# The first 256 tokens' softmax rebuilt, one more unit with narrow attention products, and a new order: a chunked-attention and channel-mix kernel on one core

## The chip, the cores and the metric

The kernel runs on one core of a Trainium2 chip. The metric is device time in microseconds (us), given as the median of several runs. A run that was recorded by the hardware profiler has a time of its own; its span, from the first to the last recorded instruction, is somewhat shorter than that time.

The engines are called as in the profile: PE (TensorE) multiplies matrices and PEld loads its weights, DVE (VectorE) does elementwise work, reductions and 32x32 transposes, ACT (ScalarE) evaluates functions and copies, POOL (GpSimd) does little here, and SP (SyncE) issues all DMA transfers through one queue, in program order.

## The reference

Inputs: q, k, v of shape (4, 8, 768, 64), eight memory keys and values per head, two mixing vectors and three weight matrices. The first half is attention in chunks of 32 tokens, each with 16 tokens of left context, 8 of right context and the 8 memory keys (64 keys in all); the second half is a channel mix with a gate.

```python
for c in range(nc):                       # 24 chunks of 32
    q_c = q[:, :, c_start:c_end]
    k_full = np.concatenate([mem_k, k[:, :, l_start:r_end]], axis=2)
    v_full = np.concatenate([mem_v, v[:, :, l_start:r_end]], axis=2)
    scores = scale * np.matmul(q_c, k_full.transpose(0, 1, 3, 2))
    scores = scores - np.max(scores, axis=-1, keepdims=True)
    a = np.exp(scores)
    a = a / (np.sum(a, axis=-1, keepdims=True) + 1e-09)
    out[:, :, c_start:c_end] = np.matmul(a, v_full)
x = out.transpose(0, 2, 1, 3).reshape(4, 768, 512)
x_prev = np.concatenate([zeros, x[:, :-1, :]], axis=1)
xk = mu_k * x + (1.0 - mu_k) * x_prev     # xr in the same way with mu_r
k = np.maximum(xk @ w_k, 0.0)             # w_k: 512 x 1024
v = k * k @ w_v                           # w_v: 1024 x 512
r = 1.0 / (1.0 + np.exp(-(xr @ w_r)))     # w_r: 512 x 512
return r * v
```

## The kernel before

**Tiles and stages.** The 3072 tokens are 12 units of 256, each of two tiles of 128 tokens (tiles 0 and 1 are unit 0, and so on). For a tile PE makes the scores s in PSUM (64 small matmuls), DVE takes the maximum of each row (mx), subtracts it (e), ACT takes the exponential of e in place, DVE sums, adds 1e-9, takes the reciprocal and multiplies ("norm"). For units 0 to 2 PE transposes e (pt, line 751), ACT and DVE copy the two halves into a zeroed block layout (aTz), and PE multiplies by v (px, line 771: 16 calls of two passes for a tile, the "wide" product). From unit 3 (MOVED) on, DVE transposes e in 32x32 blocks (eT, L900), it goes to DRAM (eD, L907) and comes back as aTz in four transfers (L911). From unit 6 (ROWX) on, px is one "narrow" product of 64 matmuls for both tiles (L843), which DVE transposes (f_turn, L850) and which comes back as xT through DRAM too (xD L856, xT L861).

From xT ACT and DVE make the two token mixes (xf: "own" on ACT, L950, and "past" on DVE, L958, for unit 0), split into a high and a low part (xh, xl). PE then makes k (ph, h in the tables of the order), the gate (pr, g) and the value products (pv, v; from unit 2 on seven products p1 to p7 into accx, accy, accz). ACT squares the relu (kf), DVE and ACT split it (ah, al), and the result o goes out.

**Weights.** Each weight arrives as 64-bit words (raw) and is joined once: ACT "abs" (L465), DVE "low" (L470), DVE "join" (L474), then a high and a low part. w0 to w3 are w_k's four blocks of 128 rows, w4 and w5 hold w_r, w6 to w9 w_v. The first product of unit 0 (ph, L1425) takes w0 as joined, with xf.

**What sets the order.** A planner (class Plan) has a cost for each operation, runs the list against its model of the engines, and writes each engine's program in the order found. LEAD lists PE's work of the first two units by hand, STAGES that of the later ones: t is a tile's transposes, a its px, s and z scores of a unit two or three ahead, x and a the px of later units. LOADS is the order of the first transfers. FORCE adds dependencies in unit 0: n, norm of tile 0 waits for the subtraction of tile 1; j, the join of w0 waits for norm of tile 1; t, the copies of tile 1's aTz both go to ACT; e would hold abs behind tile 1's exponential. FETCH and its kin model stops of PE's own instruction queue. While PE would idle before the first ph it multiplies zeros ("warm", L1639).

**The lines of unit 0.** Tile 0 is done by first_part in two halves (q0a, q0b): scores L670, maxima L679 and L681, subtraction L688 and L690, exponential L693, sums L699, L701, L702, norm L706. Tile 1 goes whole through the general path: scores L588, maximum L601, subtraction L606, exponential L612, sums L616 to L618, norm L622.

## Time and profile before

| what | us |
|---|---|
| median of 3 runs | 377.25 (374.96 to 377.32) |
| the profiled execution's own time | 376.67 |
| its span | 374.9 |
| PE busy | 367.7 (98% of the span) |
| DVE busy | 322.7 (86%) |
| ACT busy | 206.2 (55%) |
| DMA | 64.78 MB, mean 173 GB/s |

The granted TensorE clock is full in all 40 slices of the span. "Busy" is the time in which an engine has an instruction at work; for PE that includes the warm matmuls of the head. The profiled execution took 0.58 us less than the median of the runs shown.

### The profile page before, as it was taken

What the parts mean: (1) busy time and instruction counts of PE and PEld (TensorE: products, weight loads), DVE (VectorE), ACT (ScalarE), POOL (GpSimd) and SP (SyncE); (2) the same over time, 40 slices, a digit from 0 to 9 for tenths busy, and PEclk for the clock granted to TensorE, in tenths of its full rate; (3) what the DMA queues carried; (4) which work ended last, traced back from release to release, by engine and by line L of the source; (5) the groups of instructions that cost most, each with busy time, mean ns of one, the idle gap of its engine ahead of it and who ended that gap; (6) DMA issues with size and microseconds to landing.
All of it is one profiled execution on the core that took longest, in us unless ns stands there. A gap on an engine that the chain in (4) does not pass through costs nothing.

```text
span 374.9 us, 11497 instructions
## 1 busy us (share of the span) xinstructions
PE 367.7 (98%) x5084; PEld 339.6 (91%) x5084; DVE 322.7 (86%) x524; ACT 206.2 (55%) x307; POOL 2.4 (1%) x9
## 2 busy tenths in 40 slices
PE   7999999999999999999999999999999999999996
PEld 5886579988999999999999998999999999999996
DVE  3899999999999499989699997996998988788274
ACT  2797996954774386475068157238338244156260
POOL 2000000000000000000000000000000000000000
PEclk9999999999999999999999999999999999999999
DMA  7999981324701735556692485266343340400101
GB/s 287 403 417 409 389 309 71 113 87 140 274 39 72 262 120 179 215 165 240 246 278 93 153 288 179 64 220 230 127 154 115 112 169 2 143 30 0 58 1 58
DMA packets 24146, 64.78 MB, mean 173 GB/s; under 512 B 2720, under 2 KB 10784, under 8 KB 23712
## 3 DMA queue, kind: packets, MB, share of 16 engines
q1 hardware_dynamic: 24096, 64.04, 47.8%
q8 instruction: 40, 0.66, 0.7%
q14 instruction: 10, 0.08, 0.1%
HBM read 49.88 MB, written 14.16 MB: 171 GB/s over the span
## 4 chain that ended last, share of the span: by engine, by line
PE 82%; DMA 9%; DVE 5%; SPq 1%; issue 1%; ACT 0%; DVEq 0%
PE ph L1479 26%; PE pr L1368 14%; PE accy L1270 10%; PE accx L1270 7%; PE accz L1270 6%; PE pv L1581 4%; DMA raw<-in_w_k_dram 4%; PE s L588 4%; PE ph L1454 3%; PE px L771 3%; PE px L843 2%; PE pv L1568 2%; DMA qk<-in_qk_dram 2%; DMA aTz<-eD 1%; DMA xT<-xD 1%
## 5 line engine op out<-in xcount | busy, mean ns | idle before, releaser
L1479 PE MATMUL ph<-xh,wk 128*128 128x256 f32 x320 | 89.1, 278 | 0.0
L1479 PE MATMUL ph<-xh,wl 128*128 128x256 f32 x320 | 88.0, 275 | 0.0
L1479 PE MATMUL ph<-xl,wk 128*128 128x256 f32 x320 | 88.0, 275 | 0.0
L1498 ACT ACTIVATE kf<-ph 128x512 f32<-128x512 f32 x47 | 27.6, 596 | 88.7 <-PE ph L1479 88.4
L1479 PEld LDWEIGHTS ph<-xh,wk 128*128 128x128 f32 x320 | 61.4, 192 | 0.8
L1479 PEld LDWEIGHTS ph<-xh,wl 128*128 128x128 f32 x320 | 61.5, 192 | 0.0
L1479 PEld LDWEIGHTS ph<-xl,wk 128*128 128x128 f32 x320 | 61.4, 192 | 0.0
L1215 DVE TENSOR_TENSOR al<-kf,ah 128x512 fp32r<-128x512 f32 x50 | 33.6, 679 | 1.8 <-PE accz L1270 1.6
L1368 PE MATMUL pr<-wr,xh 128*128 128x512 f32 x88 | 34.1, 388 | 0.0
L1368 PE MATMUL pr<-wr,xl 128*128 128x512 f32 x88 | 33.4, 379 | 0.0
L1368 PE MATMUL pr<-wl,xh 128*128 128x512 f32 x88 | 33.4, 379 | 0.0
L397 ACT CAST ah<-kf 128x512 fp32r<-128x512 f32 x45 | 27.3, 620 | 9.7 <-DVE kf L1193 7.2
L1505 ACT ACTIVATE kf<-kf 128x512 f32<-128x512 f32 x45 | 28.1, 632 | 1.1
L1377 ACT ACTIVATE sg_sb<-pr 128x512 f32<-128x512 f32 x24 | 14.0, 597 | 20.5 <-PE pr L1368 20.3
L1270 PE MATMUL accx<-wv,ah 128*128 128x256 f32 x80 | 22.1, 276 | 0.0
L1270 PE MATMUL accx<-wv,al 128*128 128x256 f32 x80 | 22.0, 275 | 0.0
L1270 PE MATMUL accx<-wl,ah 128*128 128x256 f32 x80 | 22.0, 275 | 0.0
L588 PEld LDWEIGHTS s<-qk 64*32 64x32 f32 x1472 | 15.2, 105 | 4.0 <-issue 2.9
L1368 PEld LDWEIGHTS pr<-wr,xh 128*128 128x128 f32 x88 | 16.7, 189 | 2.5
L1368 PEld LDWEIGHTS pr<-wr,xl 128*128 128x128 f32 x88 | 16.6, 189 | 2.3
L1368 PEld LDWEIGHTS pr<-wl,xh 128*128 128x128 f32 x88 | 16.7, 189 | 1.9
L588 PE MATMUL s<-qk 64*32 64x64 f32 x1472 | 17.2, 225 | 1.1 <-DMA qk<-in_qk_dram 1.1
(165 smaller groups left out, 956.0 us busy)
## 6 DMA issues: line engine op xcount, KB each, us to landing
qk<-in_qk_dram SPq DMA_DIRECT2D x23, 768.0 KB, 6.1
vw<-in_vw_dram SPq DMA_DIRECT2D x24, 512.0 KB, 5.2
out_dram<-o SPq DMA_DIRECT2D x23, 256.0 KB, 2.4
eD<-eT SPq DMA_DIRECT2D x9, 512.0 KB, 2.7
aTz<-eD SPq DMA_DIRECT2D x36, 128.0 KB, 3.0
raw<-in_w_v_dram SPq DMA_DIRECT2D x4, 1024.0 KB, 10.2
raw<-in_w_k_dram SPq DMA_DIRECT2D x3, 1024.0 KB, 10.6
xD<-aTz SPq DMA_DIRECT2D x6, 512.0 KB, 2.6
```

Of the source, the lines that this page charges most:

```text
L397: e.copy(dst, src)
L588: nc.tensor.matmul(s5[CHUNK * j : CHUNK * (j + 1), h, d - c, r, :], *operands(ts[d], r, j, slice(64 * h, 64 * h + 64)), start=True, stop=True,
L771: nc.tensor.matmul(p3[64 * h : 64 * h + 64, 2 * g : 2 * g + 2, CHUNK * j : CHUNK * j + CHUNK], v[:, g, h, j, :], a[:, h, g, j, :], start=True,
L1215: nc.vector.tensor_sub(low(n), place[n](), T["ah", u, n].bitcast(F32))
L1270: nc.tensor.matmul(o, x, w, start=(n in fresh and c + i == 0), stop=(c == cs[-1] and i == 2), skip_group_check=True)
L1368: nc.tensor.matmul(pairs(p), x[:, place_of(u)[k], c * P : (c + 1) * P], woven(w), start=(k + n == 0), stop=(k == KT - 1 and n == 2),)
L1377: nc.scalar.activation(sg, p, AF.Sigmoid)
L1454: nc.tensor.matmul(pairs(T["ph", u, f][:, i * UTOK : (i + 1) * UTOK]), w[:, fc], x[:, :, k].rearrange("p t n -> p n t"), start=(i + k + n ...
L1479: nc.tensor.matmul(pairs(p[:, i * UTOK : (i + 1) * UTOK]), w[:, fc], x[:, :, place_of(u)[k]].rearrange("p t n -> p n t"), start=(k + n == ...
L1498: e.activation(part(), p, AF.Relu)
L1505: e.activation(q, q, AF.Square)
L1581: nc.tensor.matmul(pairs(p), x[:, tc_], woven(w), start=(f + n == 0), stop=(f == FT - 1 and n == 2),)
```

## The change

In the first_part of the new kernel:

- Tile 0 is FUSED: DVE takes the maxima and multiplies them by -SCALE; ACT then takes the exponential straight from PSUM in eight instructions of 128 x 64, each with its own column of maxima as bias and with the row sum as a second output (accum_out). DVE's two subtractions and two sums of tile 0 are gone.
- Tile 1 is loaded in two halves (q1a, q1b) and goes through maxima, subtraction, exponential and sum in two halves.
- Tile 0's scores lie in two banks of tag m and two of tag tp.

Beyond first_part: FORCE is "njc" (c makes w0's abs wait for tile 0's copies; t is gone, so one of tile 1's copies may go to DVE); ROWX is 5, so unit 5 has the narrow px; LOADS, LEAD and STAGES are new, and so is the model of queue stops and one more kind of edge when the order is written (a slot's opener behind its last opener).

```diff
-FORCE = "njt"
+FORCE = "njc"
-LOADS = "q0a q0b q1 id w0 v0 v1 w1a w1b w2 w4 w3 q3 q2 w5 w6 v2 w7 w8 v3 q4 w9 q5"
+FUSED, FUSED_US = (0,), 1.2
+LOADS = "q0a q0b q1a q1b w0 id v0 v1 w1a w1b w2 w3 q2 w4 q3 w5 w6 w7 v2 w8 w9 v3 q4 q5"
 STAGES = {
...
-    10: "h0 h1 h2 h3 p1 p7 g0 p6 p4 p5 p2 p3",
+    9: "h0 h1 x h2 h3 p1 z g0 p7 p6 g1 p5 p2 p4 p3",
+    10: "h0 h1 h2 h3 g0 p1 p7 p6 p4 p5 p2 p3",
...
-ROWX = 6
+ROWX = 5
...
-FETCH, FETCH_LEAD, FETCH_US, FETCH_AT, FETCH_FROM, FETCH_RATE = 256, 40, 4.9, 123, 2600, (0.0046, 0.0088)
+FETCH, FETCH_LEAD, FETCH_US, FETCH_AT, FETCH_FROM, FETCH_RATE = 256, 32, 4.0, 123, 2600, (0.0046, 0.0088)
...
+                elif k > b:
+                    marks[b] = max(marks.get(b, 0.0), ready)
...
+                if s.tag in opened and opened[s.tag] is not o:
+                    edge(opened[s.tag], o)
+                opened[s.tag] = o
...
+            def f_sub(b):
+                if fused:
+                    nc.vector.tensor_scalar_mul(mxs(b), mxs(b), -SCALE)
+                    return
...
+            def f_exp(b):
+                if not fused:
+                    nc.scalar.activation(e4(b), e4(b), AF.Exp, scale=SCALE)
+                    return
...
+                for h in range(2):
+                    for r in range(R):
+                        g = slice(R * b + r, R * b + r + 1)
+                        nc.scalar.activation(
+                            e4(b)[:, h, r], s4(b, h)[:, r], AF.Exp, bias=pt["mx"][:, h, g], scale=SCALE, accum_out=pt["sum"][:, h, g]
+                        )
...
+            es_, banks = [], [[Slot("s")]] * 2 if t else [[Slot("m"), Slot("m")], [Slot("tp"), Slot("tp")]]
```

How the engines' programs stand before and after, at three places. In the names, e is the exponentials' tile, s_0_0 to s_0_3 are tile 0's score banks, mx_0, sum_0 belong to tile 0, mx_1, sum_1, s_1 to tile 1; a wait is named by the engine whose count is waited for.

ACT at the start of the program, before:

```order
L693 ACT_TABLE_LOAD
L693 ACTIVATE e_136<-e_136 128x2x128 [waits DVE_49] x2
L612 ACTIVATE e_136<-e_136 128x2x256 [waits DVE_49]
L465 ACTIVATE w_208<-raw_187 128x512 [waits DMAHW5_49]
L397 COPY aTz<-pt_199 64x512 [waits PE_49]
L397 COPY aTz<-pt_199 64x512
L465 ACTIVATE w_208<-raw_187 128x512
L397 COPY aTz<-pt_223 64x512 [waits PE_49]
L397 COPY aTz<-pt_223 64x512
```

and after (the rows left out are the second instruction of each pair and one abs with its copy):

```order
L715 ACT_TABLE_LOAD [waits DVE_49]
L715 ACTIVATE e_140,sum_0_139<-s_0_0_92,mx_0_117 128x64 [waits PE_49]
L715 ACTIVATE e_140,sum_0_139<-s_0_0_92,mx_0_117 128x64
L715 ACTIVATE e_140,sum_0_139<-s_0_1_94,mx_0_117 128x64 [waits PE_49]
...
L715 ACTIVATE e_140,sum_0_139<-s_0_2_96,mx_0_117 128x64 [waits DVE_49,PE_49]
...
L715 ACTIVATE e_140,sum_0_139<-s_0_3_98,mx_0_117 128x64 [waits PE_49]
...
L706 ACTIVATE e_140<-e_140 128x2x128 [waits DVE_49] x2
L473 ACTIVATE w_218<-raw_188 128x512 [waits DMAHW4_49]
L405 COPY aTz<-pt_208 64x512 [waits PE_49]
...
L405 COPY aTz<-pt_224 64x512 [waits DVE_49]
```

The table load, which stood unwaited, now stands behind a wait for DVE; two exponentials of tile 0 have become eight that read PSUM; tile 1's has become two of half the width; and one copy of tile 1's aTz is left on ACT, behind a DVE instruction.

DVE from the last step of tile 0's softmax to w0's join, before (two sums of tile 0 stand ahead, L699):

```order
L601 TENSOR_REDUCE mx_1_189<-s_1_148 128x8 [waits PE_49]
L606 TENSOR_TENSOR e_136<-s_1_148,mx_1_189 128x2x256 [waits DVE_49]
L706 TENSOR_TENSOR e_136<-e_136,sum_0_143 128x2x256
L616 TENSOR_REDUCE sum_1_204<-e_136 128x8 [waits Activation_49]
L617 TENSOR_SCALAR sum_1_204<-sum_1_204 128x8 [waits DVE_49]
L618 RECIPROCAL sum_1_204<-sum_1_204 128x8 [waits DVE_49]
L622 TENSOR_TENSOR e_136<-e_136,sum_1_204 128x2x256 [waits DVE_49]
L470 TENSOR_SCALAR raw_187<-raw_187 128x1024 [waits DMAHW5_49]
L474 SCALAR_TENSOR_TENSOR w_208<-w_208,raw_187 128x1024 [waits DVE_49,Activation_49]
```

and after (six maxima, two scalings and tile 1's first subtraction stand ahead):

```order
L726 TENSOR_SCALAR sum_0_139<-sum_0_139 128x8 [waits Activation_49]
L727 RECIPROCAL sum_0_139<-sum_0_139 128x8 [waits DVE_49]
L700 TENSOR_TENSOR e_140<-s_1_147,mx_1_170 128x2x128
L724 TENSOR_REDUCE sum_1_200<-e_140 128x2x2 [waits Activation_49]
L731 TENSOR_TENSOR e_140<-e_140,sum_0_139 128x2x256 [waits DVE_49]
L724 TENSOR_REDUCE sum_1_200<-e_140 128x2x2 [waits Activation_49]
L726 TENSOR_SCALAR sum_1_200<-sum_1_200 128x8 [waits DVE_49]
L727 RECIPROCAL sum_1_200<-sum_1_200 128x8 [waits DVE_49]
L731 TENSOR_TENSOR e_140<-e_140,sum_1_200 128x2x256 [waits DVE_49]
L478 TENSOR_SCALAR raw_188<-raw_188 128x1024 [waits DMAHW4_49]
L407 COPY aTz<-pt_224 64x512 [waits PE_49]
L482 SCALAR_TENSOR_TENSOR w_218<-w_218,raw_188 128x1024 [waits DVE_49,Activation_49]
```

Tile 0's add and reciprocal now wait for ACT and stand between tile 1's two subtractions; tile 1's steps come in halves; a copy of aTz (L407) stands between low and join.

SP where unit 8's probabilities go to DRAM and come back, before (eD_3206 and aTz; qk are later score operands):

```order
L907 DMA eD_3206<-eT_3204 128x1024
L561 DMA qk_3212<-in_qk_dram 128x1536
L911 DMA aTz<-eD_3206 32x4x256 x4
L561 DMA qk_3297<-in_qk_dram 128x1536
L745 DMA vw_3307<-in_vw_dram 128x1024
...
L856 DMA xD_3369<-aTz 128x1024
```

and after (eD_3214 is the same transfer):

```order
L945 DMA eD_3214<-eT_3211 128x1024
L1353 DMA out_dram<-o_0_2810 128x512
L949 DMA aTz<-eD_3214 32x4x256 x4
L569 DMA qk_3235<-in_qk_dram 128x1536
...
L783 DMA vw_3377<-in_vw_dram 128x1024
...
L894 DMA xD_3418<-aTz 128x1024
```

The qk load that stood between eD and the four aTz transfers now stands behind them, and an output stands there.

PE in unit 1 and 2, at the transposes and products of tiles 4 and 5 (pt_830, px_860 are tile 4; pt_836, px_885 tile 5; of the twelve ph rows between, four are shown), before:

```order
L751 MATMUL pt_830<-id_sb,e_738 128x128 x4
L751 MATMUL pt_836<-id_sb,e_738 128x128 x4
L1454 MATMUL ph_2_780<-xh_0_683,wk_71 128x256
L1454 MATMUL ph_2_780<-xl_0_685,wk_71 128x256
L1454 MATMUL ph_2_780<-xh_0_683,wl_736 128x256
...
L1454 MATMUL ph_3_787<-xh_0_683,wk_71 128x256
...
L771 MATMUL px_860<-aTz,vw_571 64x2x32 x16
L771 MATMUL px_885<-aTz,vw_575 64x2x32 x16
L1368 MATMUL pr_0_909<-wr_76,xh_1_772 128x512
```

and after (pt_952 is tile 5's transposes, px_959 and px_987 are the products of tiles 4 and 5; tile 4's transposes stand 27 rows higher up):

```order
L1406 MATMUL pr_0_929<-wr_77,xh_1_797 128x512
L1406 MATMUL pr_0_929<-wl_909,xh_1_797 128x512
L1406 MATMUL pr_0_929<-wr_77,xl_1_840 128x512
L789 MATMUL pt_952<-id_sb,e_745 128x128 x4
L809 MATMUL px_959<-aTz,vw_656 64x2x32 x16
L809 MATMUL px_987<-aTz,vw_658 64x2x32 x16
L1619 MATMUL pv_0_1007<-wv_72,kh_0_829 128x512
L1619 MATMUL pv_0_1007<-wl_942,kh_0_829 128x512
```

The twelve ph products that stood between tile 5's transposes and the px products are ahead of the transposes now.

## Rows read from the trace of the kernel before

**Rows 1.** Busy time by stretch: from:to, length, then PE, PEld, DVE, ACT, POOL

```profile
0.00:16.56 16.56, 13.87 (x229) 10.62 (x229) 9.54 (x25) 6.97 (x12) 2.33 (x8) 1.00 0.90 338
16.56:220.00 203.44, 203.33 (x2950) 183.54 (x2947) 188.58 (x287) 129.34 (x191) 0.11 (x1) 1.00 0.58 208
220.00:226.00 6.00, 4.82 (x55) 4.50 (x62) 4.58 (x9) 4.21 (x8) 0.00 (x0) 1.00 0.69 211
226.00:374.90 148.90, 145.71 (x1870) 140.97 (x1868) 119.99 (x206) 65.69 (x99) 0.00 (x0) 1.00 0.31 104
```

**Rows 2.** Waits from 220 to 228: total us, times, longest

```profile
PE px L843 <- DMA aTz<-eD: 1.2, 2, 0.6
```

**Rows 3.** SP's transfers around unit 8's eD: start, us of issuing

```profile
215.22 0.33 SPq L907 DMA_DIRECT2D eD<-eT  x1
215.60 0.45 SPq L561 DMA_DIRECT2D qk<-in_qk_dram  x1
218.12 2.88 SPq L911 DMA_DIRECT2D aTz<-eD  x4
```

**Rows 4.** The chain that ended last, in order of time: start, us, piece

```profile
1.64 6.87 DMA qk<-in_qk_dram
...
67.23 1.34 PE ph L1454 x12
68.58 2.02 PE px L771 x64
...
174.06 1.41 PE px L843 x89
...
220.56 5.28 DMA aTz<-eD
```

**Rows 5.** The timeline of the first 17 us: start, us, instruction [idle before]

```profile
0.73 1.28 ACT L693 ACT_TABLE_LOAD   x1 [0.73 <-PEq L1685]
...
4.80 0.49 DVE L679 TENSOR_REDUCE mx<-s 128x2 f32<-128x128 f32 x2 [3.41 <-PE s L670]
...
5.74 0.42 DVE L681 TENSOR_REDUCE mx<-s 128x4 f32<-128x256 f32 x1
...
8.64 0.85 PE L588 MATMUL s<-qk 64*32 64x64 f32 x64 [1.08 <-DMA qk<-in_qk_dram]
...
9.53 0.69 DVE L601 TENSOR_REDUCE mx<-s 128x8 f32<-128x512 f32 x1 [1.55 <-PE s L588]
...
12.81 0.69 DVE L622 TENSOR_TENSOR e<-e,sum 128x512 f32<-128x512 f32 x1
13.41 0.69 DVE L470 TENSOR_SCALAR raw<-raw 128x1024 uint32<-128x1024 uint32 x1
...
14.26 1.23 DVE L474 SCALAR_TENSOR_TENSOR w<-w,raw 128x1024 uint32<-128x1024 uint32 x1
...
15.93 0.35 DVE L958 SCALAR_TENSOR_TENSOR xf<-px,mu_sb,xf 128x127 f32<-128x127 f32 x1 [0.44 <-ACT xf L950]
...
16.56 12.03 PE L1425 MATMUL ph<-xf,w 128*128 128x128 f32 x68
```

**Rows 6.** ACT's timeline, 17 to 52 us

```profile
17.85 0.37 ACT L950 ACTIVATE xf<-px,mu_sb 128x128 f32<-128x128 f32 x1
18.11 0.67 ACT L465 ACTIVATE w<-raw 128x512 f32<-128x512 f32 x1
...
41.61 0.19 ACT L785 COPY xT<-xT 128x4 f32<-128x4 f32 x1
...
49.14 1.28 ACT L1377 ACT_TABLE_LOAD   x1
50.44 1.08 ACT L1377 ACTIVATE sg_sb<-pr 128x512 f32<-128x512 f32 x2
```

**Rows 7.** DVE's timeline at tile 5's copy and at unit 4's transpose

```profile
67.27 0.68 DVE L399 COPY aTz<-pt 64x512 f32<-64x512 f32 x1
...
116.26 1.24 DVE L900 STREAM_TRANSPOSE eT<-e 128x1024 f32<-128x1024 f32 x1
```

More of the change, by code (lines that the diff above doesn't have):

```diff
@@ L158, in place, with fetched @@
         return best
-    def fetched(self, t, cost, n):
+    def fetched(self, t, cost, n, ready):
         d = self.count - FETCH_FROM
@@ L216, in edge @@
             need[b] += 1
-        follows, prev, waits = {}, {}, {}
+        follows, prev, waits, opened = {}, {}, {}, {}
         for o in done:
@@ L720, in scores @@
+            else:
+                prior.update(norm=o_n)
+            return o_s, [o_n]
         qs = [Slot(big("q", t)) for t in ts]
@@ L722, in scores @@
         for t, x in zip(ts, qs):
-            if t == 0:
-                l.append([op(("dma", 1.05), lambda b=b: f_load(0, b), new=[x] * (b == 0), use=[x] * b, due=0.1 * b) for b in range(2)])
-                loads.update(q0a=l[0][0], q0b=l[0][1])
+            if u == 0:
+                l.append([op(("dma", 1.05), lambda b=b, t=t: f_load(t, b), new=[x] * (b == 0), use=[x] * b, due=0.2 * t + 0.1 * b) for b in range(2)])
+                loads.update({f"q{t}a": l[t][0], f"q{t}b": l[t][1]})
             else:
@@ L731, in scores @@
         for c in range(0, QPU, step):
-            o_s, o_n = first_part() if u + c == 0 else part(c, step, o_s, u > 0)
+            o_s, o_n = first_part(c, o_s) if u == 0 else part(c, step, o_s, u > 0)
             done += o_n
@@ L796, in attention @@
         da = due.get(("a", t), 0.0)
-        lv = loads[f"v{t}"] = op(("dma", 1.35), f_loadv, new=[vs], lat=3.3 if u > 3 else DLAT)
+        lv = loads[f"v{t}"] = op(("dma", 2.05 if t == 1 else 1.35), f_loadv, new=[vs], lat=3.3 if u > 3 else DLAT + 0.3 * (t == 1))
         if u >= MOVED:
```

152 lines of the change are left out of this document (81 added, 71 removed), and 10 rows, old and new, of the table STAGES.

## The prediction

> **What bounds the kernel now.** I read the busy time by stretch first [rows 1]. From 16.56 us on PE is at work for 203.33 of 203.44 us up to 220, for 4.82 of 6.00 between 220 and 226, and for 145.71 of the last 148.90, where the rest is the last output. So the time is a head of 16.56, then PE's own work, then one hole of about 1.2, then a tail that no edit touches. DVE and ACT are less busy in every stretch, so what the change gives them costs or saves nothing unless PE comes to wait for it. Three questions are left: when the first ph starts, how much PE work there is, and which holes close or open.
>
> The waits put the hole at unit 8's px, which waits 1.2 for aTz to come back from DRAM [rows 2]. SP's transfers show what led to it: eD goes out at 215.22, a qk load is issued at 215.60 while eD is under way, and the four aTz reads follow at 218.12 [rows 3]; the last of them takes 5.28 from 220.56 in the chain [rows 4].
>
> The head I read from the timeline [rows 5] and the chain [rows 4]. Tile 1's operands take 6.87 us from 1.64, so its scores start at 8.64. DVE then has an almost unbroken run from the maximum at 9.53 to the norm that ends at 13.50, low until 14.10, join from 14.26 to 15.49 and the last mix at 15.93, whose end (16.28) lets the first ph go at 16.56. ACT loads its table at 0.73, long before it has data.
>
> **The change part by part.** The sum is made against the profiled execution, 376.67, of which the span is 374.9; the median of the runs shown, 377.25, lies 0.58 above it.
>
> *Unit 5's narrow product.* A wide px takes 2.02, a narrow one 1.41 [rows 4], both as PE time in the chain: **−0.61**. It adds one DVE transpose and the trip through DRAM. For a transpose of that size I take 1.24 [rows 7]; it lies under PE's products, as do the transfers, because unit 5's mix is wanted only a whole unit later. If that cover were gone, PE would wait for xT; that belongs to the rival of a new hole, below.
>
> *The hole at 220 to 226.* In the new order the qk load stands behind the four aTz reads, with only a small output in front. The 1.2 then goes, or stays if the reads are slow for another reason: that the qk load slows them is my reading, since nothing else is issued between. I take **−1.2**, bounds 0 and −1.2. If the reads land earlier, little is late next: after 226 PE idles for 3.19 in all, and 2.9 of that is the tail [rows 1].
>
> *Tile 5's px.* Before, twelve ph products (1.34 [rows 4]) lie between tile 5's transposes and px, and hide the copies of aTz. Now px of tile 4 follows the transposes at once, which covers half a wide pair, 1.01 [rows 4], and tile 5's px waits for its copies: a DVE copy of 0.68 [rows 7], which starts behind an ACT copy's worth of other work (another 0.68 at most), so 1.36 or so. **+0.4**, bounds 0 (another copy engine free) and +0.7. Nothing is lost beyond it, as the ph products were done earlier.
>
> *A later output step.* In unit 2 a value product waits for a PSUM bank that DVE frees; the new order puts eT of unit 4, 1.24 long [rows 7], in front of that freeing add. Bounds 0 and +0.9; nearest row is the transpose itself, less what PE has to do meanwhile. I take **+0.2**.
>
> *The head, tile 1's side.* Before, DVE needs 3.97 from the end of the scores to that of the norm: five steps of 0.69 and 0.52 for add and reciprocal with their gaps [rows 5]. Now five half steps at 0.42 (what a maximum of half the width takes, at 5.74 [rows 5]), two norms at 0.69 and add and reciprocal twice, 0.52 each, make 4.52: +0.55. Against that the scores end earlier: the first half's are done when the second half's operands land, which saves half of 0.85, 0.43. The norm of tile 1 so ends 0.1 late, near 13.6. Then DVE has one more instruction between low and join, a copy of aTz, which both went to ACT before. Low ends near 14.2, the copy 0.68 later at 14.9, join (1.23) near 16.1, the mix (0.35) near 16.5, and the first ph 0.28 behind it as before, 16.75. **+0.2**, bounds −0.7 (tile 1's halves land earlier than 8.5 and DVE's whole run moves up) and +0.5.
>
> *The head, ACT's side.* Here the trace of before has no row for the new instruction. ACT's table load now stands behind a wait for DVE's scaled maxima: those end near 5.5 (maxima from 4.80, 0.49 for two, plus a scaling that I take at 0.2), the load takes 1.28, so the first exponential starts near 6.8 instead of 5.7. Eight follow. The step from one ACT instruction with a column as operand to the next is 0.26 for 128 x 128 (17.85 to 18.11 [rows 6]); reading out a column sum cannot be less than nothing, nor, I think, dearer than a whole tiny copy, 0.19. So a step lies between 0.26 less the smaller width, say 0.21, and 0.37 + 0.19 = 0.56, where nothing overlaps. I take 0.35, near the pair that overlaps plus half of a read-out. Then the eight end near 6.8 + 8 x 0.35 = 9.6. DVE wants the sums at about 9.9 (9.07 for the scores' end, then two half steps of 0.42), so there is 0.3 in hand: **0**. Above a step of 0.38 the cover is gone, and each 0.1 more moves add, reciprocal and all DVE work behind them, tile 1's too, by 0.8. At 0.56 that is +1.45; at 0.21 nothing is gained, as DVE is busy anyway. One engine's wait is thus the price of the whole first part.
>
> On the table load the profile has two cases [rows 5, 6]: at 0.73 with no work behind it, and at 49.14, where a load of 1.28 is followed by the next instruction at 50.44, 0.02 after its end. The Trainium skill, "ScalarE: Activation LUTs", section "What ACT_TABLE_LOAD costs", puts a switch at about 1283 ns for the load and a further 1380 ns for a drain. The load agrees; no drain shows behind it at 49.14. By that rule the exponentials would start 1.38 later and the sum would come to 376.8; the same case, worked out from rows, is a rival below.
>
> *No price.* w3 ahead of w4, q2 and q3 between them, the banks for tile 0 and the planner's model of queue stops change order only; PE shows no stop of that kind after 16.56 that a new order could remove (0.11 idle in 203.44 us [rows 1]).
>
> The sum: −0.61 − 1.2 + 0.4 + 0.2 + 0.2 + 0 = −1.01, so 376.67 − 1.01 = **375.7**.
>
> **The rivals.**
> - *The eight exponentials set the head.* Slower than before. Place: the add after tile 1's second maximum, which waits for ACT. It decides from a step of 0.38 on, and turns the sign at 0.38 + 1.01 / 8 = 0.51. At the upper bound, 0.56, the time is 375.66 + 1.45 = **377.1**. For it: a read-out as a second instruction, eight times, and the late table load. Against it: ACT's instructions overlap in the row at 17.85.
> - *The first exponential doesn't follow the load at once.* If it came one more load's length late, 1.28, the eight would end at 10.9, past 9.9 by 1.0: **376.7**. Against it, the 0.02 between 49.14 and 50.44 [rows 6]. Its place is the same add; it differs from the case above by idle time ahead of the first exponential.
> - *The hole stays.* The chain of eD and aTz stays as slow for another reason, or another moved unit's aTz or xT comes late where STAGES has changed: 375.66 + 1.2 = **376.9**. For it: DMA share 0.69 in that stretch against 0.58 before it [rows 1], and the order of every stage has changed. Against it: the qk load is gone from where it stood.
> - *Tile 1's operands land earlier.* In halves, with w0 behind them, they may land before 8.5, and all of DVE's run moves up by up to 0.7: **375.0**. Against it: the bytes ahead are the same, and DMA's share is 0.90 already in the head [rows 1].
> - *The change doesn't do what it says*, since tile 0's own steps were never on the path (DVE was idle 1.55 before tile 1's maximum [rows 5]). Tile 1's run alone then sets the head, as in my forecast, and the eight exponentials buy nothing: within **375.7** again, so it gets no chance of its own.
>
> **How the numbers follow.** Forecast 375.7: 0.40. Exponentials set the head, 377.1: 0.18. A late first exponential, 376.7: 0.07. The hole stays or another opens, 376.9: 0.20. Operands earlier, 375.0: 0.15. All lie within 1% of 377.25, which is 3.77 us and about what a measurement of this kernel can tell from no change. The range runs from 375.0 less 1.2, half of what the runs shown differ by (374.96 to 377.32), so 373.8, to 377.1 plus the 0.65 by which the highest run shown lies above the profiled one, so 377.8. A gain over 3.8 needs several terms that I don't see: 0.11. A loss over 3.8 needs a step above 0.9 or a wait of whole transfers: 0.07. The rest, 0.82, is no change that shows.
>
> **What would show it.** Right: the first ph starts between 16.3 and 17.0; eight exponentials of at most 0.38 from start to start, done before DVE's add; unit 5's px at 1.41; PE without idle time from 220 to 226; a wait of 0.3 to 0.5 ahead of tile 5's px. Wrong: DVE waits for ACT before the add; idle time between the table load and the first exponential; a wait of px for aTz or of a mix for xT in any unit from 5 on; a head that ends before 15.9 or after 17.2; PE stops that no wait explains.

## The result and the profile after

| what | before, us | after, us |
|---|---|---|
| median of 14 runs each | 375.70 (374.92 to 377.32) | 377.95 (376.60 to 381.06) |
| ratio after / before | | 1.0064 (95% interval 1.0043 to 1.0085) |
| profiled execution, its span | 376.67, 374.9 | 379.85, 378.1 |

The kernel became slower by 0.64% in the ratio, by 2.25 us in the medians; the forecast was a small gain. The three runs shown ahead of it had a median 1.5 us above that of all fourteen, so that the forecast of 375.7 is by chance the time of the kernel before.

The busy time of after in the stretches of [rows 1] (its columns as there):

```profile
0.00:17.74 17.74, 14.82 (x220) 11.13 (x220) 9.37 (x28) 8.31 (x27) 2.76 (x8) 1.00 0.92 351
17.74:220.00 202.26, 200.66 (x2985) 179.91 (x2982) 188.43 (x288) 125.67 (x185) 0.11 (x1) 1.00 0.58 208
220.00:226.00 6.00, 6.00 (x57) 6.00 (x56) 5.73 (x10) 3.20 (x6) 0.00 (x0) 1.00 0.59 160
226.00:378.10 152.10, 147.72 (x1888) 142.67 (x1886) 121.60 (x206) 67.15 (x104) 0.00 (x0) 1.00 0.32 110
```

The hole between 220 and 226 is closed: PE is at work for 6.00 of 6.00, as forecast. But the head ends at 17.74 where it ended at 16.56, PE idles 1.60 between 17.74 and 220 where it had idled 0.11, and there is a new hole behind 226. PE's waits from 18 to 374 us name them (total us, times, longest), beside the one row of before [rows 2]:

```profile
PE px L881 <- issue: 1.3, 1, 1.3
PE px L881 <- DMA aTz<-eD: 0.5, 1, 0.5
PE pt L789 <- DVE e L630: 0.5, 1, 0.5
PE px L809 <- DVE aTz L407: 0.3, 1, 0.3
```

L789 is the transposes, L809 the wide and L881 the narrow product of the new file. The chain of after shows the last, the second and the first of these places (start, us, piece):

```profile
75.25 0.70 DVE aTz L407
...
76.00 1.15 PE px L809 x32
...
134.65 8.25 DMA eD<-eT
...
144.24 3.08 DMA aTz<-eD
...
147.46 1.46 PE px L881 x86
...
229.05 1.33 PE px L881 x84
230.38 1.34 issue
231.72 0.32 PE px L881 x9
```

At 75.25 tile 5's px waits for its copy on DVE. At 147.46 unit 5's narrow product takes 1.46, near the 1.41 of the forecast, but behind a wait: its eD took 8.25 to land, where unit 8's took 2.88 in before. SP had issued two loads of vw just ahead of it (start, us of issuing):

```profile
133.05 1.27 SPq L783 DMA_DIRECT2D vw<-in_vw_dram  x2
134.65 0.33 SPq L945 DMA_DIRECT2D eD<-eT  x1
```

This looks like the hole of before at another unit, with vw in place of qk; no run here moves these loads. At 230.38 PE stops for 1.34 near the end of unit 8's narrow product: of its 128 passes (64 matmuls, two passes each in the trace; the chain lists only a part of them) 119 are done, nine are to come, and no semaphore is waited for. The transfer of the program's own instructions has a row in the view of DMA queues, here from 229.3 to 231.75 (packets, MB, share): one packet, which the trace starts at 229.43.

```profile
q8 instruction: 1, 0.02, 0.7%
```

The head of after, in the timeline of all engines, against [rows 5]:

```profile
5.62 1.28 ACT L715 ACT_TABLE_LOAD   x1 [5.62 <-DVE mx L693]
...
6.92 0.32 ACT L715 ACTIVATE e<-s,mx 128x64 f32<-128x64 f32 x1
...
7.13 0.19 ACT L715 ACTIVATION_READ_ACCUMULATOR e<-s,mx 128x1 f32 x1
7.23 0.31 ACT L715 ACTIVATE e<-s,mx 128x64 f32<-128x64 f32 x1
...
7.55 0.68 PE L674 MATMUL s<-qk 64*32 64x64 f32 x32 [0.69 <-DMA qk<-in_qk_dram]
...
8.16 4.63 PE L1677 MATMUL warm<-zero_sb 128*128 128x256 f32 x10
...
9.43 0.17 DVE L726 TENSOR_SCALAR sum<-sum 128x8 f32<-128x8 f32 x1 [0.35 <-ACT e L715]
...
10.37 0.68 DVE L731 TENSOR_TENSOR e<-e,sum 128x512 f32<-128x512 f32 x1
...
11.86 0.69 DVE L731 TENSOR_TENSOR e<-e,sum 128x512 f32<-128x512 f32 x1
...
12.59 1.06 PE L789 MATMUL pt<-id_sb,e 128*128 128x128 f32 x4
...
16.86 0.35 DVE L996 SCALAR_TENSOR_TENSOR xf<-px,mu_sb,xf 128x127 f32<-128x127 f32 x1
...
17.74 0.94 PE L1463 MATMUL ph<-xf,w 128*128 128x128 f32 x6
```

Two things are to be seen. DVE waits 0.35 for the sums of the eight exponentials, which come 0.29 apart. And tile 0's norm is done at 11.05, but the transposes that want it stand on PE behind ten passes over zeros which take 0.43 each; in the head of before ten such passes took 2.43 from 9.42. That is the granted clock, although the row of the head prints it as 1.00. The trace's list of clock stretches begins only at 13.71 us in this profile, at 6.45 in the one of before, and the views count time without an entry as full; so "full in all 40 slices" says nothing about the first microseconds. At 13.71 the warm passes step from 0.43 to 0.22. A later profile, of a kernel with the same head but for a few small products (the small shift below, profiled again), has the lower level on record, 0.50 or 1.2 GHz of 2.4 (the last column but two):

```profile
7.80:11.10 3.30, 3.30 (x47) 2.77 (x42) 2.53 (x8) 2.18 (x12) 0.00 (x0) 0.50 1.01 391
11.20:13.60 2.40, 2.40 (x16) 2.10 (x15) 1.76 (x5) 1.23 (x2) 0.33 (x2) 1.00 1.02 413
```

Its warm passes take 0.43 from 9.19 to 11.06 and 0.22 after. In before, PE passes the time until tile 1's operands land with six more warm passes; after has none there, and PE idles 0.43 and 0.69 ahead of tile 1's two score groups:

```profile
5.59 1.97 PE L1639 MATMUL warm<-zero_sb 128*128 128x256 f32 x6
```

Since tile 1's operands land at another time in each execution (the scores end at 9.49 in this profile of before and at 7.81 in the next, at 8.23 in this one of after), heads are compared below from **the end of tile 1's last scores to the first ph**, called the head: 7.07 before, 9.52 after.

### The profile page after: what moved, and what is told of

Read it like the earlier page. It is cut to its first block, busy times and chain, and to the rows that moved or that the text cites. A ratio compares the mean times of both kernels' runs of the same rounds, so it can differ in the third digit from the quotient of the medians.

```text
span 378.1 us, 11618 instructions
## 1 busy us (share of the span) xinstructions
PE 369.2 (98%) x5140; PEld 339.7 (90%) x5140; DVE 325.1 (86%) x529; ACT 204.3 (54%) x319; POOL 2.9 (1%) x9
## 4 chain that ended last, share of the span: by engine, by line
PE 84%; DVE 7%; DMA 4%; ACT 2%; issue 1%; SPq 1%
PE ph L1517 25%; PE pr L1406 13%; PE accy L1308 10%; PE accx L1308 6%; PE accz L1308 6%; PE pv L1619 4%; PE ph L1463 3%; PE s L596 3%; PE ph L1492 3%; PE px L881 3%; DMA eD<-eT 2%; PE pv L1606 2%; PE px L809 2%; PE warm L1677 2%; DMA qk<-in_qk_dram 1%
## 5 line engine op out<-in xcount | busy, mean ns | idle before, releaser
L405 ACT CAST ah<-kf 128x512 fp32r<-128x512 f32 x49 | 29.6, 621 | 18.3 <-DVE kf L1231 12.2
L1543 ACT ACTIVATE kf<-kf 128x512 f32<-128x512 f32 x46 | 28.9, 632 | 2.4 <-DVE kf L1538 1.2
L609 DVE TENSOR_REDUCE mx<-s 128x16 f32<-128x1024 f32 x11 | 13.5, 1224 | 4.1 <-PE s L596 3.9
```

Of the source, the lines that this page charges most:

```text
L405: e.copy(dst, src)
L609: nc.vector.reduce_max(mx, s4(), axis=AX.X)
L1543: e.activation(q, q, AF.Square)
```

## The experiments

Four theories stood at the start, and most of them may hold together: the sums of tile 0 come late, since the table load waits (theory D in the expectations); PE's slow warm passes hold the transposes back (A); the stop at 230 belongs to a place in PE's instruction stream, which any shift of the stream moves (E); and, the rival of all (C), what one profile shows belongs to that execution alone. Ratios are against the runs of before beside which each kernel ran.

**Both kernels once more.** No edit.

> The kernel before, profiled a second time. Theory C (the hole of 1.2 us at unit 8's narrow product belongs to one execution, not to the kernel): PE's idle time after the first ph is under 0.5 us and the run takes about 375.5. Rival (the hole is the kernel's own, as the prediction had it): the same product waits 1.0 to 1.3 us for aTz again, near 224 us, and the run takes about 376.7. Both expect the first ph at 16.4 to 16.7.

> The changed kernel, profiled a second time. Theory C: the stop of 1.34 us inside the narrow product at 230 and the 0.54 us at 147 are gone or elsewhere, PE's other idle time stays (0.5 ahead of tile 2's transposes near 39, 0.3 at tile 5's px near 76), and the run takes about 378. Rival (a stop fixed by the order of the instructions): 1.3 us again at the same product, about 379.8. Both expect the first ph at 17.6 to 17.9.

Measured: 376.17 and 377.93. Before has its hole at unit 8 again, 1.21, and its 7.07 from scores to ph. After has its stop again, 1.07 at 228.72 with the same nine passes of the product to come, so theory C falls for both. The ten warm passes took 2.42 this time, and the head was still 8.57: in this execution DVE was ready for the sums at 8.30 and PE was not in the way. Its row on DVE's timeline:

```profile
9.38 0.17 DVE L726 TENSOR_SCALAR sum<-sum 128x8 f32<-128x8 f32 x1 [1.08 <-ACT e L715]
```

Between these two profiles PE's last instruction ends 2.00 later: the first ph 1.13, idle time behind the first ph 0.68 (2.01 before, 2.69 after, in gaps over 0.1), PE's own work 0.19.

**The rate of the warm passes.** One small product of zeros goes ahead of each of two score groups, so that PE has something to do while operands land:

```diff
+    fill = {2: 128, 3: 192}
...
+                if pes in fill:
+                    c = fill.pop(pes)
+                    nc.tensor.matmul(warm[:, :c], zero_sb[:, :P], zero_sb[:, :c], start=True, stop=True)
+                pes += 1
```

> The changed kernel with two small products of zeros more: 128 columns ahead of tile 1's first half of scores, 192 ahead of its second half, in gaps where PE idled for 0.44 and 0.69. Theory A (the ten warm passes at 0.43 each hold tile 0's transposes back, because PE had not yet stepped up to its faster rate): the step to 0.22 a pass comes before 9 us, the warm passes end near 10.7, tile 0's transposes start at 11.1 instead of 12.6, and the first ph at 15.8 to 16.3 instead of 17.74; about 376.2. Theory B (the rate does not matter; w0's first step, now queued behind tile 0's copies, and the DVE copy ahead of the join make the head late): the first ph stays at 17.4 or later, about 378.

The other way, at most three warm products (six passes) in a row:

```diff
+                n = min(n, 3)
```

> The changed kernel with three products of zeros (six passes) ahead of tile 0's transposes instead of five (ten). Theory A: the passes stay at 0.43 but end near 10.9, so tile 0's transposes start at 11.1 and the first ph comes at 16.2 to 16.6, about 376.7. Theory B: the first ph stays at 17.4 or later, about 378.

Measured: 377.38 (376.85 to 379.42, 12 runs; ratio 1.0049, 1.0032 to 1.0066) with the fill, and 379.07 (377.71 to 380.12, 6 runs; 1.0085, 1.0054 to 1.0116) with three passes. PE's timeline with the fill:

```profile
7.47 2.43 PE L1682 MATMUL warm<-zero_sb 128*128 128x256 f32 x10
11.25 0.63 PE L789 MATMUL pt<-id_sb,e 128*128 128x128 f32 x4 [1.35 <-DVE e L731]
```

The ten passes take 2.43 and PE waits for DVE, as it should; scores to ph is 8.45, 1.07 less than in the first profile of after. With three products PE is free early, but the transposes themselves then take 1.08 instead of 0.63 (the list of clock stretches begins at 14.07), and the head is 8.24. Over all profiles of new heads in halves the ten (or fourteen) passes, or what is left of them, ran wholly or partly at the slow rate in six of seven without the fill, and in one of seven with it, the last below. The trace's list of clock stretches says the same: with the fill it begins between 4.0 and 6.0 us in all seven, and falls back in that one; without it, it begins at 13 to 14 us in four, falls back to 0.50 near 7.9 in two, and is early and stays in one. So theory A holds, and the slow rate is the lower granted clock. The fill is worth about 1 us of the head in the executions that have it.

**The table load.** A one-column exponential of zeros, whose result nothing uses, lets ACT load its table at the start; alone, then with the fill:

```diff
+    early = const.tile([P, 1], F32, tag="early", name="early")
+    nc.scalar.activation(early, zero_sb[:, 0:1], AF.Exp)
```

> The changed kernel with one tiny exponential of a zeroed column at the very start of ACT's program (its result is not used), so that the table load runs near 1 us and not behind DVE's scaled maxima at 5.6. Theory D (where tile 1's operands land early, as in both second profiles, DVE's add waits for the eight exponentials, and these start 1.3 late because of the load): the first exponential starts near 5.6, DVE's wait of 1.08 ahead of the add goes, the first ph comes about 1.0 earlier relative to the landing, and the time falls by 0.5 to 1.1, to 376.9 to 377.4. Rival (the exponentials' own step of 0.29 or the copy of aTz on DVE sets the head): less than 0.3 gained, 377.6 or more.

> The kernel of e3 (two small products of zeros in the gaps between the first score groups) with the early table load of e5 added. In e5 PE was still at its slower rate until 12 us and the ten warm passes hid what the load was worth; here they should not. Theory D: DVE no longer waits for ACT ahead of tile 0's add, tile 0's transposes start near 10.2 instead of 11.25, the first ph near 14.9 instead of 15.99, and the time falls by 0.8 to 1.1 against e3, to 376.3 to 376.6. Rival (DVE's own run and the copy of aTz set the head): the first ph comes at 15.5 or later, less than 0.5 gained, 376.9 or more.

Measured: 378.72 (377.23 to 380.51, 6 runs; 1.0095, 1.0070 to 1.0120) alone: the exponentials start at 5.59, but the slow warm passes (4.63 for ten) hide it, and the head is 9.52 as in after. With the fill 377.61 (376.38 to 379.14, 12 runs; 1.0050, 1.0028 to 1.0071). There DVE doesn't wait any more:

```profile
8.75 0.41 DVE L691 TENSOR_REDUCE mx<-s 128x4 f32<-128x256 f32 x1
9.08 0.16 DVE L728 TENSOR_SCALAR sum<-sum 128x8 f32<-128x8 f32 x1
```

and the head is 7.45, 1.00 less than with the fill alone. But tile 1's scores end 0.75 later here (8.29 against 7.54), and the first ph comes only 0.25 earlier. Without the early load the first ph stands at 16.00, 15.99 and 16.05 in three profiles with the full clock, whether these scores end at 7.43, 7.54 or 8.54: ACT's exponentials set it. With the early load it follows the scores, by 7.45, 7.79 and 7.39 where they end at 8.29, 7.47 and 8.58 (the last two are profiles of the kernel below that has the small shift, the early load and tile 5's transposes moved). So the late sums cost 0.7 where tile 1 lands early (8.45 against 7.79) and nothing where it lands late (7.51 against 7.45 and 7.39), the slow passes 1.07, and 0.3 to 0.7 is left for the halves and the copy on DVE. This is one reason why the early load gained nothing in the median (377.61 against 377.38); whether it is the only one is not shown.

**Tile 0 not fused, tile 1 whole.** In the first kernel tile 0 has its subtractions and sums on DVE again, in the second tile 1 goes as before, with one load (the line that does it; the others name the load and keep FORCE's dependencies):

```diff
-FUSED, FUSED_US = (0,), 1.2
+FUSED, FUSED_US = (), 1.2
```

> The changed kernel with tile 0's softmax as before (subtraction, exponential and sums in halves on DVE and ACT), all other parts of the change kept. Theory D: DVE gets 1.7 us of instructions back, but no longer waits for ACT; the table load runs at 0.73 again; the first ph comes 0 to 0.6 earlier than in the changed kernel, 377.4 to 378.0. Rival (the eight exponentials relieve DVE, which sets the head): the first ph comes 0.5 to 1.0 later, about 378.7.

```diff
-            o_s, o_n = first_part(c, o_s) if u == 0 else part(c, step, o_s, u > 0)
+            o_s, o_n = first_part(c, o_s) if u + c == 0 else part(c, step, o_s, u > 0)
```

> The changed kernel with tile 1 loaded whole and its softmax in whole steps as before; tile 0's fused exponentials and all else as in the change. The prediction's term for the halves was +0.1 on tile 1's norm: then the first ph comes within 0.2 of the changed kernel's relative to the landing of tile 1, about 378. Rival F (the halves put tile 0's add and reciprocal, and a second score bank's wait, into the middle of DVE's run, and the ten warm passes or ACT's eight steps then hold it up; whole steps give ACT time): the first ph follows the last landing by 0.5 to 1.0 less, and about 377.2.

Measured: 381.05 (380.14 to 381.59, 4 runs; 1.0151, 1.0135 to 1.0168) without the fused exponentials, 11.08 from scores to ph. DVE gets its four half steps back, but that is not all: fourteen warm passes, at a granted clock of 0.50 from 7.88 to 11.29, hold tile 0's transposes to 12.82, and the planner has put a copy of tile 0's aTz ahead of tile 1's norm, which so starts at 14.79. With fusing the time is 3.1 lower in the medians; how much of that is fusing itself, and what the half steps cost, this run doesn't show. Tile 1 whole: 377.68 (376.75 to 378.61, 12 runs; 1.0052, 1.0035 to 1.0070), head 8.93, because DVE's add still waits for the eight exponentials and tile 1's maximum, whose scores end at 7.85, stands behind it:

```profile
9.28 0.17 DVE L730 TENSOR_SCALAR sum<-sum 128x8 f32<-128x8 f32 x1 [2.93 <-ACT e L719]
...
9.61 0.64 DVE L609 TENSOR_REDUCE mx<-s 128x8 f32<-128x512 f32 x1
```

Taking out either half of the head's edit doesn't bring the 7.07 back.

**The stop without a semaphore.** If it belongs to a place in the stream, the kernel before must get such stops from a shift alone. Two of the five warm products ahead of tile 0's transposes become 25 tiny ones, which makes PE's stream 92 places longer (each pass is two entries, a load of weights and a multiplication) and changes nothing behind it:

```diff
+                if n == 5:
+                    n = 3
+                    for _ in range(25):
+                        nc.tensor.matmul(warm[0:CHUNK, :NK], zero_sb[0:64, :CHUNK], zero_sb[0:64, :NK], start=True, stop=True)
```

> The kernel before with two of its five warm products ahead of tile 0's transposes replaced by 25 tiny ones, so that PE's stream is longer by 92 places ahead of everything else; nothing else differs on any engine. Theory E (where PE's dense groups fall in its stream decides whether it runs dry): stops of 1 to 2.6 us that no semaphore explains appear at one or more score groups or narrow products, and the time rises by 1 to 6 us. Rival (in e10 the early load and the moved transposes were to blame): within 0.5 of before, 375.6, with no new stop.

Measured: 386.94 (385.16 to 389.20, 4 runs; 1.0320, 1.0277 to 1.0363). The chain of this kernel:

```profile
177.57 1.34 PE px L843 x85
178.91 1.60 issue
...
198.63 1.28 PE px L843 x81
199.90 3.35 issue
```

There is a third stop of 1.30 at 33.82, so the three make 6.25 where before has none. The edit isn't free in the head either: the tiny products take 3.34 from 9.46 and, with the warm passes behind them, hold the transposes to 14.13, and the head is 9.29 instead of 7.07. Against the second profile of before PE's last instruction ends 9.1 later: 1.9 by the landing of tile 1, 2.2 by the head, 5.1 by idle time (the stops, less waits of before that are gone), less 0.1 or so of PE's own work. The same shift in after, with the fill, the early load and tile 5's px of below:

> The kernel of e9 with tile 5's transposes moved up as in e8, and with two of the five warm products ahead of tile 0's transposes replaced by 25 tiny ones of zeros (32 x 64), so that every later instruction of PE stands 92 places further back in its stream, at no cost in time. Theory E (the stop of 1.07 to 1.45 in unit 8's narrow product belongs to a fixed place in PE's stream, number 6849 of the recorded ones in six profiles, where the stream runs dry, and not to the product): the stop falls on another part of the product and shrinks or goes, 0.5 to 1.2 less; with 0.3 from tile 5's px the time is about 375.2 if e9 gives 376.4. Rival (the product waits for something of its own): the same stop of 1.1 to 1.4 after the same matmul of the product, and 376.1.

Measured: 388.05 (385.29 to 390.63, 6 runs; 1.0319, 1.0273 to 1.0365). The stop near 228 is gone, and two others have come: 1.76 in the scores at 121.72 and 2.63 in accx at 172.36. Behind both the granted clock falls, from 124.2 to 127.6 and from 175.4 to 178.8 (the clock is the last column but two):

```profile
124.20:127.60 3.40, 3.40 (x19) 3.40 (x18) 1.06 (x1) 0.00 (x0) 0.00 (x0) 0.50 0.94 277
```

So a stop can cost more than its length; behind the stop of 3.35 above, the clock did not fall. The three runs of the shifted before that were not profiled had a mean clock of 0.990 or 0.991, which its profile, at 0.999, had not. Now a shift of 20 places more than the fill's, which should leave the stop in the product but nearer to its start:

```diff
+                if pes == 5:
+                    for _ in range(5):
+                        nc.tensor.matmul(warm[0:CHUNK, :NK], zero_sb[0:64, :CHUNK], zero_sb[0:64, :NK], start=True, stop=True)
```

> The kernel of e3 with five tiny products of zeros ahead of the warm ones, so that PE's stream is longer by 20 places (28 against the changed kernel). In twelve profiles every stop of PE without a semaphore stands at a place whose number in the recorded stream is 193 more than a multiple of 256, and place 6849 falls near the end of unit 8's narrow product in the changed kernel. Theory E: place 6849 moves 28 places towards the product's start, the stop falls from 1.1-1.4 to under 0.5 (0.42 in e13, which is 14 places longer), no other grows, and the time falls by 0.7 to 1.0 against e3, to about 376.5. Rival (the stop's size has nothing to do with how much of the product stands ahead of the place): 1.1 to 1.4 again, 377.4.

> The kernel of e15 with the early table load of e5 and tile 5's transposes moved up as in e8: all that the experiments found to cost time in the changed kernel and that can be undone without undoing the change. If the parts add up: e15 less 0.3 for tile 5's px, less 0 to 1.0 for the load, 375.3 to 376.2, about the time of the kernel before. Rival (the head of the changed kernel is longer for its own reasons, by 0.4 from the last score to the first ph, and a wait of 0.5 ahead of tile 2's transposes stays): 376.2 or more.

Measured: 377.45 (375.66 to 379.28, 12 runs; 1.0050, 1.0025 to 1.0076), and 377.72 (375.07 to 378.48, 12 runs; 1.0042, 1.0017 to 1.0067) with the early load and tile 5's px as well. In the profiles, 376.21 and 375.17, the stop is down to 0.43 and 0.26; in the second the chain reads

```profile
225.46 1.21 PE px L883 x76
226.67 0.26 issue
226.93 0.42 PE px L883 x23
```

Counting all entries of PE's stream in the trace, every stop over 0.15 us that the trace puts down to no semaphore, in every kernel, lies at a number that leaves 193 when it is divided by 256, but for the one in the run with a table for stage 6 (below):

| place | product | stops, us |
|---|---|---|
| 961 | pr | 1.30 (before, shifted) |
| 3265 | s | 1.76 (after, shifted) |
| 3777 | s | 0.09 to 1.09 (seven profiles with after's order) |
| 5057 | px; accx | 1.60 (before, shifted); 2.63 (after, shifted) |
| 5825 | px | 3.35 (before, shifted) |
| 6849 | px | 1.34, 1.07 (after); 0.26 to 1.96 (others) |

(Three more, at 5569, 6593 and 7361, are of 0.11 to 0.28.) The place 6849 stayed where streams grew by 8, 14 and 28 entries, while the pass of the product at which PE stopped moved: 9, 13, 16 and 23 of the 128 were to come. Each time a packet of queue 8 (16 KB, "instruction") starts 2.2 to 2.6 us before PE goes on. A place in a dense small product is not enough for a stop: the kernel before has thirteen such places in s and px from 125 us on and no stop; in its first profile the packet had started 3.4 us or more ahead of each. I read this as PE running ahead of its instructions. The Trainium skill, "Runtime: NRT & Kernel Launch", section "Instruction fetch mechanics", says that instructions come in 16 KiB blocks of 256, the next while the current one is executed, and that crossing a boundary is mostly hidden. Blocks of that size and spacing are what the trace shows; hidden the boundaries are not at the places of the table, most of them in or behind products whose 128 small passes take 1.4 us, by up to 3.35 us a time.

The twelve times of each of these two kernels fall into two groups: 375.66 to 376.71 (6) and 378.19 to 379.28 (6); 375.07 to 375.57 (4) and 377.49 to 378.48 (8). Both profiles are of the lower group, so each kernel ran once more for a profile of the upper one.

> The kernel of e16 profiled a second time. Its twelve times fall in two groups, 375.07 to 375.57 and 377.49 to 378.48, and its profile was of the lower one. Theory E (a block of PE's stream that just arrives in time in the one group comes too late in the other): a profile of the upper group shows one or two stops of 1 to 2.5 us in all, without a semaphore, at places 193 more than a multiple of 256. Rival A (PE's slower rate in the head): a step of 0.43 for the warm passes until 11 us or later, and the first ph 2 us later after the last score. A profile of the lower group (about 375.2) leaves it open.

> The kernel of e15 profiled a second time, for the same question: its times fall into 375.66 to 376.71 and 378.19 to 379.28. Theory E: in the upper group one or two stops of 1 to 2.5 us in all at places 193 more than a multiple of 256. Rival A: the slower rate in the head, first ph 2 us later. A profile near 376.2 leaves it open.

Measured: 375.83, just above its lower group, and 377.74, just below its upper one. In the latter PE's warm passes ran in part at the lower granted clock, which had been full from 4.34 and was 0.50 from 7.75 to 11.16 (2.43 would be the time at full clock), and the stop was 0.67:

```profile
9.19 3.38 PE L1685 MATMUL warm<-zero_sb 128*128 128x256 f32 x10
```

The head took 8.77 against 7.51 in the other profile of this kernel. The clock in the head thus explains 1.3 of the 1.5 between these two executions; that it makes the whole upper group is likely, not shown. The second kernel's lower group is at the time of before, but its median, 377.72, is hardly below that of after, 377.95.

**Single terms.** Tile 5's transposes ahead of twelve ph and twelve gate products again (in LEAD):

```diff
-... t4 s3.0 h1.1.3 g1.0 t5 a4 a5 ...
+... t4 s3.0 t5 h1.1.3 g1.0 a4 a5 ...
```

> The changed kernel with tile 5's transposes moved up, to behind the scores of unit 3 and ahead of twelve ph products and twelve of the gate. The term of the prediction (+0.4 for a wait of tile 5's px, 0.32 measured near 75 us in every profile of the changed kernel): that wait is gone, 0.3 less, 377.6. Rival (PE then waits elsewhere for what DVE and ACT do later): the same time, with the idle time at another place.

Unit 5 with the narrow product in the kernel before, one line, after which the planner orders everything anew:

```diff
-ROWX = 6
+ROWX = 5
```

> The kernel before with unit 5's narrow product alone (its place on PE as before; DVE, ACT and SP are re-planned around it). By the prediction's first term PE needs 0.61 less and the rest is hidden: 375.0 where before takes 375.6. Rival (the narrow product brings its own waits for aTz, xT or the plan around it, as the 0.3 to 0.5 at unit 5's px in the changed kernel): the same time as before within 0.3, or more.

In the kernel before, unit 8's qk load behind the four aTz reads on SP, and nothing else:

```diff
+        seq = list(plan.order())
+        ins = [o for o in seq if o in T["in", 8]]
+        late = seq.pop(max(k for k in range(seq.index(ins[0])) if seq[k].eng == "dma"))
...
+        seq.insert(seq.index(ins[-1]) + 1, late)
```

> The kernel before with one move on SP and nothing else: the qk load that stood between unit 8's eD and its four aTz transfers is issued behind them. The prediction's largest term (-1.2: the hole of 1.2 us at unit 8's product, in both profiles of before, goes with that load): the product starts without a wait, PE's idle time after the first ph is under 0.3, and the time is 374.4 where before takes 375.6. Rival (the hole is not the load's, or PE's instruction stop of the changed kernel comes in its place once the product is no longer held up): 1 us or more of idle time within that product still, and 375.3 to 375.6.

And a stage table of its own for stage 6 of after, to move unit 8's product away from the stop:

```diff
+    6: "h0 z h1 h2 h3 p1 g0 x p7 p6 g1 p2 p5 p4 p3",
```

> The changed kernel with one order moved: in the stage of unit 6 unit 8's narrow product stands behind the first half of the gate instead of ahead of it. Theory E (the stop of 1.07 to 1.34 inside that product, which waits for no semaphore, comes from PE running out of instructions where the scores and the narrow product, each of many small instructions, stand close together): no such stop near 229 us, and 1.0 to 1.3 less, about 376.8. Rival (something else stops PE at that time, or the stop moves to the next dense place): a stop of about 1 us again within 10 us of that place, and about 378.

Measured: with tile 5's transposes moved 378.33 (377.21 to 379.46, 4 runs; 1.0071, 1.0053 to 1.0090): the wait of 0.32 at 75 us is gone from PE's waits, and the two tiles' px follow each other as 64 passes in 2.09. The term is confirmed; the median doesn't show 0.3.

With unit 5 narrow alone 381.73 (380.81 to 383.14, 6 runs; 1.0156, 1.0124 to 1.0188). Its waits:

```profile
PE px L843 <- issue: 2.0, 1, 2.0
PE pr L1368 <- DVE xh L399: 1.7, 2, 1.0
...
PE pr L1368 <- DVE xl L1032: 1.1, 2, 0.6
PE accy L1270 <- DVE o L1312: 0.8, 1, 0.8
```

The planner's new order brings a stop of 2.0 at place 6849, and DVE, with one more transpose, is late for the gate twice. Behind the stop the granted clock is 0.50 again, from 231.9 to 235.3. With the old tables the edit of ROWX is no gain of 0.6 but a loss of some 6.

With the qk load moved 375.30 (374.24 to 377.21, 12 runs) against 375.94 (23 runs): 0.9985, 0.9966 to 1.0004. The stretch of the hole:

```profile
220.00:226.00 6.00, 6.00 (x166) 5.71 (x165) 4.70 (x8) 4.46 (x8) 0.00 (x0) 1.00 0.90 316
```

The hole of 1.2 is closed by this one exchange, though the DMA share is now 0.90 there. SP issues the first aTz transfer as soon as eD has landed in both kernels (218.12 before [rows 3], 217.44 here); what differs is how long the four take. From 217 to 222 us, before (KB each, median us to landing):

```profile
aTz<-eD SPq DMA_DIRECT2D x4, 128.0 KB, 6.2
```

and with the exchange:

```profile
aTz<-eD SPq DMA_DIRECT2D x4, 128.0 KB, 3.0
```

So it was the transfer of the qk load, issued ahead of theirs, that kept aTz late, and neither SP nor the DMA engines' total load. The median gains 0.64, which the interval doesn't quite tell from nothing. No other kernel here had a lower median.

With a table for stage 6 379.09 (378.35 to 380.00, 5 runs; 1.0103, 1.0087 to 1.0120). The stop within the product is gone, but the chain has a wait in its place, and DVE's timeline shows what is late:

```profile
230.92 1.36 issue
232.28 1.58 PE px L882 x87
```

```profile
230.96 1.22 DVE L615 TENSOR_TENSOR e<-s,mx 128x1024 f32<-128x1024 f32 x1
```

The planner has also moved a subtraction on DVE, and px starts 0.1 after its end, which is likely what it waited for: the wait lies at no place of the kind above (entry 6635, which leaves 235). This run doesn't tell the theories apart.

## Why the prediction was wrong

- **"No price ... the planner's model of queue stops change order only"**: the step that failed most plainly. The trace of before could show no stop, since its order had none. The new order put place 6849 into unit 8's narrow product, where its packet came late: +1.07 to +1.34, which eats the gain at 220. A shift of the stream gave the kernel before, which had no such stop, 6.25 us of them.
- **The hole, −1.2**: right, mechanism and size; PE is busy 6.00 of 6.00, and the exchange of the issues alone does it.
- **The head, +0.2 and 0**: mis-sized. The step of the exponentials is 0.29, less than the 0.35 taken; the load takes 1.28 and the next instruction starts 0.02 later. The drain that the Trainium skill ("ScalarE: Activation LUTs", section "What ACT_TABLE_LOAD costs") adds to a table load doesn't show here. (The estimate by its rule should have been 376.7 and not 376.8: the eight would end 1.08 past 9.9.) But "DVE wants the sums at about 9.9" took one execution's landing of tile 1 as fixed. When it lands early DVE wants them at 8.30, and the exponentials end by their own clock, from the load at 5.6, near 9.35. So the rivals "the eight exponentials set the head" and "operands land earlier" came true together, the first at a step well under its 0.38, and the second couldn't pay out. And PE's clock and the warm passes had no term at all: at the lower granted clock, 0.43 each, ten of them hold the transposes to 12.59. In place of +0.2 the two pairs of profiles show +1.18 and +1.13; from the scores' end, without the luck of the landing, it is +2.45 and +1.50.
- **Tile 5's px, +0.4; the later output step, +0.2**: 0.32 and 0.13 (a gap of PE at 123.53, too short for the list of waits, which ends 0.15 behind the DVE add that frees accy), right.
- **Unit 5's narrow product, −0.61**: the product takes 1.46 and not 2.02, but waits 0.54 (0.30 in the second profile) for its aTz: 2.00 together. "A transpose lies under PE's products, as do the transfers" was right for xT and wrong for the product's own operand, whose eD landed 8.25 after its issue (8.16 in the second profile). In all, PE is busy in px for 19.86 from the first ph on before and for 19.73 after.
- **What had no term**: tile 2's transposes wait 0.5 for DVE's norm at 39.3, and PE's stream changes between lines of the kernel 113 times instead of 106. In the first pair PE's work grew by 0.48 where −0.61 was forecast, by 0.19 in the second; that the changes are what made it grow is not shown.

The sum by the second pair: first ph +1.13, idle time +0.68 (the hole of before gone, −1.21, and a wait of 0.80 for a weight's join at 25.95 that before has only where its first ph comes early; the stop, tile 2, tile 5, unit 5's product and smaller ones in their place), work +0.19, that is +2.00 of the 2.25 between the medians.

What stays open: why the granted clock rises late or falls back in the head of some executions only, what makes the upper group of times, and why the medians show so little of what the fill, the early load and the small shift gain in the profiles.

## What to carry to other kernels

An order of instructions that comes out of a planner has no price of zero: where PE runs dense small matmuls, look up which of them hold a place 256 entries apart in its stream, and what a few entries more ahead of them would do, before any edit is costed. Cost a wait in the head against the earliest landing seen, not against the one in the profile, and ask what fills PE meanwhile: small products of zeros in the gaps brought the full clock earlier here, but passes that only fill time must not stand ahead of work that is ready. Before a row's full clock is believed, look where the trace's record of it begins, and compare the time of like passes. And try the part of a change that has one clear mechanism by itself: here the exchange of two transfers was the only one that didn't lose.

## What the hardware showed

Inserting 92 entries into PE's stream, with the same work behind them, raised the median by 11 us; in the profile 6.25 of it were stops of 1.30 to 3.35 us, at places a multiple of 256 entries apart, and 2.2 the head. Behind three stops of 1.76 to 2.63 us the granted clock fell to 0.50. Ten warm passes of one kind took 2.42 or 4.63 in two executions of one kernel: 0.22 each at a granted clock of 1.00, 0.43 at 0.50, and 0.43 in the first microseconds of every profile, for which the trace has no clock on record. An exponential with a row sum is two instructions on ACT, and yet the next starts 0.29 to 0.31 after the one ahead (128 x 64), since the read-out of 0.19 to 0.24 lies beside the next one's start.
